# Attention beside an FFN: exponentiating and transposing each tile's probabilities in the step that rounds them, and splitting them one step behind

## The chip, the cores and the metric

One Trainium2 chip, one of its cores. The metric is the device time of one execution in microseconds (us), lower is better. The engines are TensorE (PE; its weight loads are PEld), VectorE (DVE), ScalarE (ACT), GpSimd (POOL) and SyncE (SP, which here only issues DMAs). Each engine runs its own queue of instructions in order and waits on semaphores for the others.

## The reference

Attention with a hash mask over 4 batches x 8 heads, 768 positions of 64 channels, whose result, all heads side by side, goes through an FFN of 512 -> 2048 -> 512 over 3072 tokens. All in float32.

```python
q_bits = (einsum('bhsd,dk->bhsk', q, proj) > 0)      # 6 bits per query, the same for keys
mask   = q_bucket[:, :, :, None] == k_bucket[:, :, None, :]
scores = where(mask, q @ k^T / sqrt(64), -1e9)
attn   = exp(scores - max(scores)); attn /= sum(attn) + 1e-9
x      = (attn @ v) as [3072, 512]
h      = x @ w_in
out    = (h * clip(h + 3, 0, 6) / 6) @ w_out
```

## The kernel before

The work of attention goes in 192 **steps** (`NS`), one for each tile of 128 queries of a head: 6 steps to a head (`KT`), 48 to a batch (`HK`). For tile `g`, in this order:

- `scores(g)` (L362, L364): 4 matmuls give the negated scores `s`, 128 queries x 768 keys, in PSUM. Products of float32 precision are made of rounded high and low parts; the hash bits ride along as extra rows, so that keys of another bucket get a huge value.
- `lowest(g)` (L371, DVE): one pass that caps `s`, writes it to the SBUF tile `p` and gives the row minimum `m`. There are two `p` tiles.
- `exponential(g)` (L383, ACT): `p = exp(m - p)` in place, with the row sum (a second instruction reads the accumulator).
- From step 106 on (`GT`) the tile is transposed by `flip(g)` and `move(g)`: a DVE transpose of 32 x 32 blocks in place (L404), a DMA of `p` to DRAM (`fd`), and four DMAs back that put the blocks in order, into one of two **homes**: the tile `spare` for even `g`, `px` for odd. Before step 106 TensorE transposes instead (`transp`, L393).
- `split_p(g, c, ...)` for the two halves c of the keys: a rounded copy `ph` (L450, ACT) and the rest `pl`, a subtraction of `ph` from the home. In these steps `pl` of c=0 is made by DVE (L454; both its inputs are in SBUF), `pl` of c=1 by POOL (L452).
- `values(u, c)` (L474, L475): 12 matmuls for a pair u of tiles, `ph` and `pl` with the head's `vv`, into `acc`; `output` copies `acc` to SBUF (L502; L499 and L500 for the last head of a batch) and sends it to the DRAM array `xs`.

The FFN of a chunk of 256 tokens runs as 16 **FFN steps**, one beside each attention step once its batch is done: `gemm1` (12 matmuls, L592 to L594) gives `h`; `gate` is a Relu on ACT (L612) and a product on DVE (L613); `split_g` makes `gh` (L620, ACT) and `gl` (L621, POOL); `gemm2` (6 matmuls, L630 to L632) adds into `po`. At a chunk's end its result is stored (L646) and the next chunk's `x` is normalised and split (L530, L540, L543, L583, L584).

PE, DVE, ACT and POOL run in the order in which the code is written (`tc.manual_schedule`); only the place of SP's DMAs is chosen by the framework. `beside_ffn(k)` writes step k of the paced part, k from 105 on. The FFN is a generator, and `go("A")` to `go("D")` let it write its next piece if that is its turn: A `split_g`, B `gemm1`, C `gemm2` of the FFN step before and then `gate`, D side work of the next chunk. Before the change step k writes: the values of a pair, `exponential(k+1)`, A, `split_p` of tile k - 2 (`LT = 2`), B, `lowest(k+2)`, `flip(k+1)`, `output`, in one step of six `hash_qk` and `bits` (the next head's hash, L316 to L318 and L327), C, `lead(k+3)` (scores, and loads and splits of the next head: L296, L304, L342, L343), the delayed DVE subtractions (`split_lows`), `move(k)`, D. `s` has one buffer, which the hash's `z` shares; `ph` and `pl` have two pairs; `fd` has four.

Of the kernel before, what the change touches and what calls it, by code (L numbers as in the profile page):

```python
# [28 lines left out]
LA = 3  # L29
FB = 4  # L30
FS = 4
FT = 6
LT = 2
WL = 30
WE = 8
WA = 4
# [7 lines left out]
def lsh_attention_moe(  # L44
# [14 lines left out]
    KT = S // P  # L59
# [16 lines left out]
    def dma(out: bass.AP, in_: bass.AP):  # L76
        nonlocal last
        last = nc.sync.dma_start(out=out, in_=in_)

    paced = False  # L80
# [146 lines left out]
    NJ = B * H  # L227
    NS = NJ * KT
# [3 lines left out]
    GT = GF + FT  # L232
# [133 lines left out]
    def lowest(g: int):  # L366

        s = scs.pop(g)
        m = sp.tile([P, 1], F32, name=f"m{g}", tag="m", bufs=4)
        pr_ = sp.tile([P, 2, HW], F32, name=f"p{g}", tag="p", bufs=2)  # L370
        nc.vector.tensor_scalar(  # L371
            out=pr_[:], in0=s[:, :, :HW], scalar1=CAP, scalar2=None,
            op0=ALU.min, op1=ALU.min, accum_out=m[:],
        )
        probs[g] = pr_, m

    def exponential(g: int):
        i, t = divmod(g, KT)
        b, h = divmod(i, H)
        if b not in sms:  # L380
            sms[b] = sp.tile([P, KT, H], F32, name=f"sms{b}", tag="sms", bufs=2)
        pr_, m = probs[g]
        nc.scalar.activation(  # L383
            pr_[:], pr_[:], AF.Exp, bias=m[:], scale=-1.0, accum_out=sms[b][:, t, h : h + 1]
        )
# [15 lines left out]
    def flip(g: int):  # L401
        nonlocal written
        x = probs.pop(g)[0][:].rearrange("p c k -> p (c k)")
        nc.vector.transpose(x, x)  # L404
        d = dp.tile([P, S], F32, name=f"fd{g}", tag="fd", bufs=4)
        dma(out=d[:], in_=x)
        written[g] = d, last
# [18 lines left out]
    def split_p(g: int, c: int, third: bool):  # L426

        nonlocal halves
        u, w = divmod(g, 2)
        if w == 0:  # L430
            extra = third and halves % 3 == 2
            halves += 1
            if extra and lent:
                both = [x[:, :S] for x in lent]
            else:
                both = [
                    sp.tile([P, NCC * TC if extra else S], F32R, name=f"{x}{u}_{c}", tag=f"x{x[1]}" if extra else x, bufs=1 if extra else 2)[:, :S]
                    for x in ("ph", "pl")
                ]
            parts[u, c] = [x.rearrange("p (x w q) -> p x w q", x=QT, w=2) for x in both]  # L440
        hi, lo = (x[:, :, w] for x in parts[u, c])
        engine = nc.vector
        if g < GT:
            pt = pts.pop((g, c))[:]
        else:
            pt = moved[g].rearrange("p (i x a) -> p x i a", i=4, x=KT)[:, c * QT : (c + 1) * QT]
            hi, lo = (x.rearrange("p x (i a) -> p x i a", i=4) for x in (hi, lo))
            if c:
                engine = nc.gpsimd
        nc.scalar.copy(hi, pt)  # L450
        if engine is nc.gpsimd:
            engine.tensor_sub(lo, pt, hi.bitcast(F32))  # L452
        else:
            lows.append(lambda: engine.tensor_sub(lo, pt, hi.bitcast(F32)))  # L454
# [3 lines left out]
    def split_lows():  # L458
        for f in lows:
            f()  # L460
        lows.clear()
# [87 lines left out]
    def multiply():  # L549
        for f in muls:  # L550
            f()
        muls.clear()
# [434 lines left out]
    vnext = 0  # L987
# [21 lines left out]
    with tc.manual_schedule(engines={ET.PE, ET.DVE, ET.Activation, ET.Pool}):  # L1009
        split_qk(0, None)  # L1010
        hash_qk(0)
        bits(0)
        scale_q(1)
        split_v(0)
        for x in range(3):
            ahead(0, x)
        for _ in range(2):
            cv(0)
        def go(part: str):
            if stage == part:  # L1020
                next(fill, None)

        through = []

        def beside_ffn(k: int):

            nonlocal paced, stage
            for c in range(2):  # L1030
                if k < GT:
                    transp(k, c)
            for _ in range(1 if k < GT else 2):
                u = vnext // 2
                if u < NS // 2 and (k < GT or k % 2 == 0 and k >= 2 * u + 2 + (LT if 2 * u >= GT else 0)):
                    if value_half():
                        through.append(vnext // 2 - 1)
            if k + 1 < NS:
                exponential(k + 1)
            go("A")  # L1040
            late = k if k < GT else k - LT
            if GT <= late < NS or k < GT:
                for c in range(2):
                    split_p(late, c, False)
            go("B")
            if k == NS + LT:
                homes.clear()
            if k + 2 < NS:
                lowest(k + 2)
            if k + 1 < NS:  # L1050
                flip(k + 1)
            paced = True
            multiply()
            while through and (through[0] < vnext // 2 - 1 or k % 2 or k < GT):
                output(through.pop(0))
            if k + LA < NS and (k + LA) % KT == 3 and (k + LA) // KT + 1 < NJ:
                hash_qk((k + LA) // KT + 1)
                bits((k + LA) // KT + 1)
            go("C")
            if k + LA < NS:  # L1060
                lead(k + LA)
            split_lows()
            if GT <= k < NS:
                move(k)
            if subs:
                subs.pop(0)()
            go("D")
            if k % KT in (2, 4):
                add()

        for k in range(NS + LT + 2):
            if k >= GT - 1:
                beside_ffn(k)
                continue
            end = GB if k < GB else NS
            i, t = divmod(k, KT)
            if k == HK - XE:
                lent += lents[cc3:]
            if k == GB:
                lent.clear()  # L1080
            if k == HK:
                late["x"] = sp.tile([P, S], F32, name="late", tag="raw", bufs=1)
            for c in range(2):
                transp(k, c)
            if k + 1 < end:
                exponential(k + 1)
            if k + 2 < end:
                lowest(k + 2)
            if k == GB:
                next(first)  # L1090
                pair_turn = 0

            third = True
            whole = False
            for _ in range(1 if k != HK else 2):
                if vnext < k - k % 2:
                    whole = value_half()
            if k >= GF - 2:
                next(fill, None)
            if whole and k >= GF:  # L1100
                output(vnext // 2 - 1)
                whole = False

            hashed = k >= GF and (k + LA) % KT == 2
            if k >= GF and k + LA < end and not hashed:
                lead(k + LA)
            for c in range(2):
                split_p(k, c, third)
            split_lows()
            if (k < GF or hashed) and k + LA < end:  # L1110
                if hashed:
                    if (k + LA) // KT + 1 < NJ:
                        hash_qk((k + LA) // KT + 1)
                        bits((k + LA) // KT + 1)
                    next(fill, None)
                lead(k + LA)
            if whole:
                output(vnext // 2 - 1)
            if k >= GF - 2 and not hashed:
                next(fill, None)  # L1120
            if k < GB:
                for f in early_steps[k]:
                    f()

            if k < HK and t == 1 and i:
                with tc.issue_after(last.ins):
                    load_w(i)
            if k == HK:
                late_x()
                with tc.issue_after(last.ins):  # L1130
                    get_qk(H + 2)
                    for n in range(WE, WL):
                        load_w(n)
            if k + 1 == GB:
                first = first_ffn(lambda part: ahead(GB, part))
                next(first)
                for _ in range(2):
                    whole = value_half()
                output(vnext // 2 - 1)
                next(first)  # L1140
        paced = False
        assert vnext == NS and not through
        add()
        for _ in fill:
            pass
# [47 lines left out]
```

## Time and profile before

| | |
|---|---|
| three runs | 1049.42, 1053.89 (median), 1058.02 us |
| the profiled execution | 1051.75 us, its span 1050.0 us |
| PE busy | 977.9 us, 93% of the span |
| DVE, ACT, POOL busy | 695.4, 637.3, 536.2 us |
| mean granted TensorE clock | 0.982 |
| the paced steps (first to last L404) | 416.3 to 864.0 us |
| DMA | 148.37 MB, mean 141 GB/s |

Busy time is not the whole cost: matmuls overlap, so their durations add up to more than the time from one issue to the next, and an instruction that is held by another engine's use of the memory shows as a longer one, not as a wait. In rows of the timeline the first number is the start, the second the duration, both in us, and in brackets stands how long the engine had been idle and what released it.

### The profile page before, as it was taken

The page shows a single profiled execution, that of the slowest core. Times are in us where ns is not written, and L with a number is a line of the kernel's source. Part 1 is how long each engine was busy: PE and PEld are TensorE (multiplying, and loading weights), DVE is VectorE, ACT ScalarE, POOL GpSimd, SP SyncE. Part 2 cuts the span into 40 slices and gives each one's busy share as a digit, 9 for nine tenths or more (in the row PEclk, how much of TensorE's full clock was granted, in tenths as well). Part 3 has the DMA queues.
Part 4 walks back from the last instruction along what each step waited for, and adds up shares of the span by engine and source line. Part 5 has one row for each costly group of instructions (what it writes and reads, how often), then busy time and mean ns, then how long its engine had stood idle before and what let it go on. Part 6 is the DMA issues. An engine that isn't in the chain of part 4 may idle for free.

```text
span 1050.0 us, 19259 instructions
## 1 busy us (share of the span) xinstructions
PE 977.9 (93%) x6330; PEld 883.7 (84%) x6330; DVE 695.4 (66%) x1350; ACT 637.3 (61%) x1419; POOL 536.2 (51%) x609
## 2 busy tenths in 40 slices
PE   8999999999999997898898898988889999999998
PEld 7999888888899997787788887877778888799997
DVE  7999988898499997566656665755655672233332
ACT  6889865555588886465656565655665574333332
POOL 6778725666367765456655555645665553200100
PEclk9999999999999999899999999999999999999999
DMA  4556587000244553677876777777786673101000
GB/s 127 145 143 168 149 275 273 1 1 1 75 124 113 115 129 93 201 214 204 230 209 190 210 197 212 195 215 205 204 238 189 185 214 84 41 1 41 1 21 21
DMA packets 109339, 148.37 MB, mean 141 GB/s; under 512 B 12804, under 2 KB 78724, under 8 KB 109240
## 3 DMA queue, kind: packets, MB, share of 16 engines
q1 hardware_dynamic: 104760, 141.64, 45.0%
q0 software_dynamic: 4480, 5.51, 4.7%
q8 instruction: 50, 0.82, 0.3%
q14 instruction: 49, 0.40, 0.1%
HBM read 75.76 MB, written 51.90 MB: 122 GB/s over the span
## 4 chain that ended last, share of the span: by engine, by line
PE 57%; DMA 16%; DVE 14%; issue 5%; ACT 3%; SPq 2%; POOL 2%; DVEq 0%; ACTq 0%; POOLq 0%
DMA fd<-p 9%; PE h L593 6%; PE h L592 6%; PE h L594 6%; PE pt L393 5%; PE po L632 4%; PE acc L475 4%; PE po L630 4%; PE acc L474 4%; DVE p L371 4%; PE po L631 4%; DVE pl L454 4%; DMA px<-fd 3%; PE s L364 3%; PE s L362 3%
## 5 line engine op out<-in xcount | busy, mean ns | idle before, releaser
L371 DVE TENSOR_SCALAR_CACHE_REDUCE p<-s 128x768 f32<-128x768 f32 x192 | 183.3, 955 | 156.7 <-DMA fd<-p 115.6
L383 ACT ACTIVATE p<-p,m 128x768 f32<-128x768 f32 x192 | 179.7, 936 | 30.2 <-DVE p L371 29.3
L612 ACT ACTIVATE g<-h,three 128x256 f32<-128x256 f32 x192 | 91.4, 476 | 157.6 <-PE h L594 137.3
L475 PE MATMUL acc<-pl,vv 128*128 128x256 f32 x564 | 147.2, 292 | 16.3 <-DVE pl L454 16.3
L613 DVE SCALAR_TENSOR_TENSOR g<-g,h 128x256 f32<-128x256 f32 x192 | 79.5, 414 | 123.1 <-ACT g L612 121.3
L474 PE MATMUL acc<-ph,vv 128*128 128x256 f32 x564 | 154.1, 303 | 3.2 <-DVE pl L454 3.1
L592 PE MATMUL h<-xh,w 128*128 128x256 f32 x512 | 147.1, 287 | 0.0
L594 PE MATMUL h<-xh,w 128*128 128x256 f32 x512 | 145.5, 284 | 0.0
L593 PE MATMUL h<-xl,w 128*128 128x256 f32 x512 | 145.5, 284 | 0.0
L621 POOL TENSOR_TENSOR gb<-g,gb 128x256 fp32r<-128x256 f32 x92 | 70.3, 764 | 127.1 <-ACT gb L620 125.3
L475 PEld LDWEIGHTS acc<-pl,vv 128*128 128x128 f32 x564 | 110.3, 196 | 21.9 <-DVE pl L454 21.6
L362 PE MATMUL s<-kk,qq 76*128 76x384 f32 x384 | 102.5, 348 | 15.0 <-DVE p L371 13.6
L474 PEld LDWEIGHTS acc<-ph,vv 128*128 128x128 f32 x564 | 109.5, 194 | 6.4 <-issue 2.2
L450 ACT CAST ph<-pt 128x384 fp32r<-128x384 f32 x204 | 91.4, 475 | 25.2 <-PE pt L393 13.7
L454 DVE TENSOR_TENSOR pl<-pt,ph 128x384 fp32r<-128x384 f32 x204 | 103.9, 549 | 3.0 <-ACT ph L450 2.5
L632 PE MATMUL po<-w,gb 128*128 128x512 f32 x248 | 100.4, 405 | 2.5 <-POOL gb L621 2.0
L630 PE MATMUL po<-w,gb 128*128 128x512 f32 x248 | 99.5, 401 | 2.5 <-ACT gb L620 2.5
L592 PEld LDWEIGHTS h<-xh,w 128*128 128x128 f32 x512 | 99.0, 193 | 1.6 <-DVE xr L543 0.2
L364 PE MATMUL s<-kk,qq 128*128 128x384 f32 x384 | 100.2, 342 | 0.0
L593 PEld LDWEIGHTS h<-xl,w 128*128 128x128 f32 x512 | 98.8, 193 | 1.6 <-DVE xl L584 0.2
L631 PE MATMUL po<-w,gb 128*128 128x512 f32 x248 | 98.6, 398 | 0.0
L594 PEld LDWEIGHTS h<-xh,w 128*128 128x128 f32 x512 | 98.6, 193 | 0.0
(164 smaller groups left out, 2398.1 us busy)
## 6 DMA issues: line engine op xcount, KB each, us to landing
fd<-p SPq DMA_DIRECT2D x86, 384.0 KB
spare<-fd SPq DMA_DIRECT2D x172, 96.0 KB
px<-fd SPq DMA_DIRECT2D x172, 96.0 KB
raw<-in_qkT SPq DMA_DIRECT2D x32, 384.0 KB
kk<-qq SPq DMA_DIRECT2D x62, 192.0 KB
wr<-in_w_in SPq DMA_DIRECT2D x16, 512.0 KB
wr<-in_w_out SPq DMA_DIRECT2D x16, 512.0 KB
vr<-in_v SPq DMA_DIRECT2D x32, 192.0 KB
```

Of the source, the lines that this page charges most:

```text
L362: nc.tensor.matmul(s[:, c, :HW], lhsT=q1[:KM, us], rhs=half(k1[:KM], c), start=True, stop=False)
L371: nc.vector.tensor_scalar(out=pr_[:], in0=s[:, :, :HW], scalar1=CAP, scalar2=None, op0=ALU.min, op1=ALU.min, accum_out=m[:],)
L383: nc.scalar.activation(pr_[:], pr_[:], AF.Exp, bias=m[:], scale=-1.0, accum_out=sms[b][:, t, h : h + 1])
L454: lows.append(lambda: engine.tensor_sub(lo, pt, hi.bitcast(F32)))
L474: nc.tensor.matmul(acc[:], lhsT=vv[:, kt], rhs=hi[:, x], start=(kt == 0), stop=False)
L475: nc.tensor.matmul(acc[:], lhsT=vv[:, kt], rhs=lo[:, x], start=False, stop=(kt == KT - 1))
L592: nc.tensor.matmul(hp[:], lhsT=wi[:, 0, wc], rhs=xh, start=(cc == 0), stop=False)
L593: nc.tensor.matmul(hp[:], lhsT=wi[:, 0, wc], rhs=xl, start=False, stop=False)
L594: nc.tensor.matmul(hp[:], lhsT=wi[:, 1, wc], rhs=xh, start=False, stop=(cc == NCC - 1))
L630: nc.tensor.matmul(po[u], lhsT=gh[:, us], rhs=wo[:, 0], start=(fc == 0), stop=False)
L631: nc.tensor.matmul(po[u], lhsT=gh[:, us], rhs=wo[:, 1], start=False, stop=False)
L632: nc.tensor.matmul(po[u], lhsT=gl[:, us], rhs=wo[:, 0], start=False, stop=(fc == NFC - 1))
```

## The change

In the paced part, step k now writes `lowest(k+2)`, `exponential(k+2)` and `flip(k+2)` one behind the other, ahead of B; `move(k+1)` instead of `move(k)`; and `split_p` of tile k - 1 (`LT = 1`), with its DVE subtraction in the same place instead of at the step's end. So a tile is rounded, exponentiated and transposed two steps ahead, read back a step sooner, and split one step behind the current one. The values of a pair are made on odd steps instead of even ones, `output` on even instead of odd, the hash on k % 6 == 5 instead of 0, and `bits` stands behind C. The loop has one iteration less.

```diff
-LT = 2
+LT = 1
...
-            for c in range(2):
-                if k < GT:
+            if k < GT:
+                for c in range(2):
                     transp(k, c)
-            for _ in range(1 if k < GT else 2):
+                exponential(k + 1)
+                flip(k + 1)
+            for _ in range(2):
                 u = vnext // 2
-                if u < NS // 2 and (k < GT or k % 2 == 0 and k >= 2 * u + 2 + (LT if 2 * u >= GT else 0)):
+                if u < NS // 2 and (2 * u < GT or k % 2 and k >= 2 * u + 3):
                     if value_half():
                         through.append(vnext // 2 - 1)
-            if k + 1 < NS:
-                exponential(k + 1)
+                if k < GT:
+                    break
             go("A")
+            if k + 2 < NS:
+                lowest(k + 2)
+                exponential(k + 2)
+            paced = True
+            multiply()
+            if k + 2 < NS:
+                flip(k + 2)
             late = k if k < GT else k - LT
             if GT <= late < NS or k < GT:
                 for c in range(2):
                     split_p(late, c, False)
+            split_lows()
             go("B")
             if k == NS + LT:
                 homes.clear()
-            if k + 2 < NS:
-                lowest(k + 2)
-            if k + 1 < NS:
-                flip(k + 1)
-            paced = True
-            multiply()
-            while through and (through[0] < vnext // 2 - 1 or k % 2 or k < GT):
+            while through and (through[0] < vnext // 2 - 1 or k % 2 == 0 or k < GT):
                 output(through.pop(0))
-            if k + LA < NS and (k + LA) % KT == 3 and (k + LA) // KT + 1 < NJ:
+            hashed = k + LA < NS and (k + LA) % KT == 2 and (k + LA) // KT + 1 < NJ
+            if hashed:
                 hash_qk((k + LA) // KT + 1)
+            go("C")
+            if hashed:
                 bits((k + LA) // KT + 1)
-            go("C")
             if k + LA < NS:
                 lead(k + LA)
-            split_lows()
-            if GT <= k < NS:
-                move(k)
+            if GT <= k + 1 < NS:
+                move(k + 1)
             if subs:
                 subs.pop(0)()
             go("D")
-            if k % KT in (2, 4):
+            if k % KT in (1, 3):
                 add()
```

In the rows below a number directly behind `p`, `m`, `s` or `fd` is the tile g, behind `ph` and `pl` the pair and then the half c; `g1_2_6` is FFN step 6 of a chunk. First VectorE's queue in steps 144 and 145, before:

```order
L371 TENSOR_SCALAR p146_8028,m146_8027<-s146_7980 128x768
L404 STREAM_TRANSPOSE p145_7960<-p145_7960 128x768
L327 TENSOR_SCALAR qq_25_7858<-z25_8033,thr_66,val_67 44x768
L613 SCALAR_TENSOR_TENSOR g1_2_6_8048<-g1_2_6_8048,h1_2_6_8014 128x256
L454 TENSOR_TENSOR pl71_0_8008<-spare_5400,ph71_0_8007 128x3x128
L371 TENSOR_SCALAR p147_8086,m147_8085<-s147_8055 128x768
L404 STREAM_TRANSPOSE p146_8028<-p146_8028 128x768
L500 TENSOR_TENSOR y23_0_7965<-acc70_7990,y23_0_7965 64x256
L613 SCALAR_TENSOR_TENSOR g1_2_7_8100<-g1_2_7_8100,h1_2_7_8072 128x256
L454 TENSOR_TENSOR pl71_0_8008<-px_5741,ph71_0_8007 128x3x128
```

And VectorE's queue at the same place after the change:

```order
L371 TENSOR_SCALAR p146_8032,m146_8031<-s146_8019 128x768
L404 STREAM_TRANSPOSE p146_8032<-p146_8032 128x768
L454 TENSOR_TENSOR pl71_0_7978<-px_5691,ph71_0_7977 128x3x128
L500 TENSOR_TENSOR y23_0_7932<-acc70_7954,y23_0_7932 64x256
L613 SCALAR_TENSOR_TENSOR g1_2_6_8064<-g1_2_6_8064,h1_2_6_8042 128x256
L371 TENSOR_SCALAR p147_8097,m147_8096<-s147_8071 128x768
L404 STREAM_TRANSPOSE p147_8097<-p147_8097 128x768
L454 TENSOR_TENSOR pl72_0_8104<-spare_5400,ph72_0_8103 128x3x128
L613 SCALAR_TENSOR_TENSOR g1_2_7_8130<-g1_2_7_8130,h1_2_7_8111 128x256
```

The transpose is now of the tile that the instruction ahead of it wrote (146 behind 146), and the subtraction L454 has moved from the step's end to right behind the transpose; it belongs to one tile later.

ScalarE's queue in the same two steps, before:

```order
L383 ACTIVATE p145_7960,sms3_7938<-p145_7960,m145_7959 128x768
L620 CAST gb1_2_5_8004<-g1_2_5_7974 128x256
L450 CAST ph71_0_8007<-spare_5400 128x3x128
L450 CAST ph71_1_8010<-spare_5400 128x3x128
L612 ACTIVATE g1_2_6_8048<-h1_2_6_8014,three_68 128x256
L383 ACTIVATE p146_8028,sms3_7938<-p146_8028,m146_8027 128x768
L620 CAST gb1_2_6_8066<-g1_2_6_8048 128x256
```

And ScalarE's queue after the change:

```order
L620 CAST gb1_2_5_8028<-g1_2_5_8011 128x256
L383 ACTIVATE p146_8032,sms3_7910<-p146_8032,m146_8031 128x768
L450 CAST ph71_0_7977<-px_5691 128x3x128
L450 CAST ph71_1_7980<-px_5691 128x3x128
L499 COPY y23_0_7932<-acc70_7954 64x256
L612 ACTIVATE g1_2_6_8064<-h1_2_6_8042,three_68 128x256
L620 CAST gb1_2_6_8093<-g1_2_6_8064 128x256
```

The exponential is of tile 146 where it was of 145, it stands behind the gate's cast instead of ahead of it, and the two copies `ph` follow it directly.

SyncE's queue at steps 144 and 145, before:

```order
L78 DMA fd145_8031<-p145_7960 128x768
L78 DMA kk_25_7857<-qq_25_7858 12x768
L78 DMA spare_5400<-fd144_7963 32x4x192 x4
L78 DMA fd146_8089<-p146_8028 128x768
L78 DMA xs2_127<-y23_0_7965 64x512
L78 DMA px_5741<-fd145_8031 32x4x192 x4
```

And SyncE's queue after the change:

```order
L78 DMA fd146_8036<-p146_8032 128x768
L78 DMA xs2_127<-y23_0_7932 64x512
L78 DMA px_5691<-fd145_7975 32x4x192 x4
L78 DMA xr2_0_8245<-xs2_127 128x4x256
L78 DMA fd147_8101<-p147_8097 128x768
```

In both the write of a tile is followed by the four reads of the tile before it; writes and reads are one tile further on in the same step.

## The prediction

> **What bounds the kernel now.** I read the page first, then the stage that the diff touches. The stretches view and the group of the on-chip transposes (line 404) show where that stage lies and how dense it is.
>
> ```profile
> 416.00:864.00 448.00, 399.75 (x2448) 358.27 (x2448) 276.22 (x481) 266.83 (x601) 252.04 (x276) 0.96 0.72 206
> ```
> ```profile
> L404 DVE STREAM_TRANSPOSE p<-p x86: 966/973/979, 416.3 to 864.0; 128x768 f32<-128x768 f32 x86
> ```
>
> In the stretches row, behind the length stand the busy times of PE, PEld, DVE, ACT and POOL, then the granted clock, the DMA share and GB/s. The 86 steps beside the FFN lie between 416.3 and 864.0, 85 intervals in 447.7 us, 5.27 us a step. No engine is full there: PE is busy 399.75 of 448 us at a granted clock of 0.96. So a wait sets the pace, and the view of waits and the chain of that stretch name it.
>
> ```profile
> DVE p L371 <- DMA fd<-p: 115.6, 55, 5.4
> ```
> ```profile
> by line: DMA fd<-p 19.7%; issue 7.5%; DMA px<-fd 7.1%; DVE p L371 5.2%; DVE p L404 5.1%; SPq L78 5.1%; DMA spare<-fd 3.9%; DVE pl L454 3.8%; PE acc L475 3.3%; PE h L593 3.0%; PE h L592 3.0%; PE h L594 3.0%; PE po L632 2.8%; PE po L630 2.7%;
> ```
>
> The largest wait of VectorE is `lowest` (L371) on the landing of an earlier step's probabilities in DRAM, and that transfer is the largest piece of the chain. VectorE's own rows show why:
>
> ```profile
> 601.95 0.96 DVE L371 TENSOR_SCALAR_CACHE_REDUCE p<-s 128x768 f32<-128x768 f32 x1 [1.24 <-DMA fd<-p]
> 602.84 0.08 DVE L371 DVE_READ_ACCUMULATOR p<-s 128x1 f32 x1
> 602.84 0.97 DVE L404 STREAM_TRANSPOSE p<-p 128x768 f32<-128x768 f32 x1
> 604.53 0.42 DVE L613 SCALAR_TENSOR_TENSOR g<-g,h 128x256 f32<-128x256 f32 x1 [0.72 <-ACT g L612]
> 604.87 0.55 DVE L454 TENSOR_TENSOR pl<-spare,ph 128x384 fp32r<-128x384 f32 x1
> 606.34 0.96 DVE L371 TENSOR_SCALAR_CACHE_REDUCE p<-s 128x768 f32<-128x768 f32 x1 [0.93 <-DMA fd<-p]
> 607.23 0.08 DVE L371 DVE_READ_ACCUMULATOR p<-s 128x1 f32 x1
> 607.23 0.97 DVE L404 STREAM_TRANSPOSE p<-p 128x768 f32<-128x768 f32 x1
> 608.12 0.38 DVE L613 SCALAR_TENSOR_TENSOR g<-g,h 128x256 f32<-128x256 f32 x1
> ```
>
> There are two `p` buffers. `lowest(k+2)` writes the one that `flip(k)` gave to the DMA a step ago. So one step is a loop: `lowest` 0.89, `flip` 0.97, then 606.34 - 603.81 = 2.53 us until the transfer has landed, together 4.39 us, and more whenever the transfer stands behind others (the mean is 5.27).
>
> **The change part by part.** No instruction is added or removed. What it does to that loop: `flip(k+2)` now stands in the step of `lowest(k+2)`, so the buffer that `lowest(k+2)` needs was given away two steps ago. Two steps of 4.5 us and more stand against 0.89 + 1.06 + 0.97 + 2.53 = 5.45 us of `lowest`, exponential, `flip` and landing. I cost this wait at nothing afterwards. Its cover is some 3.5 us beyond an ordinary landing (waits of 0.93 and 1.24 in the rows); only one like the longest, 5.4, would come through, with under 1 us. The question is what is late next. That is a new chain inside a step: `lowest` waits for the scores, the exponential for `lowest`, `flip` for the exponential, and behind `flip` on VectorE queue the low part of the probabilities (`pl`, L454), the gate (L613), bits, and the next `lowest`. For its times:
>
> ```profile
> 605.13 0.92 ACT L383 ACTIVATE p<-p,m 128x768 f32<-128x768 f32 x1
> 605.96 0.19 ACT L383 ACTIVATION_READ_ACCUMULATOR p<-p,m 128x1 f32 x1
> 606.05 0.39 ACT L620 CAST gb<-g 128x256 fp32r<-128x256 f32 x1
> 606.34 0.93 ACT L450 CAST ph<-px 128x384 fp32r<-128x384 f32 x2
> ```
> ```profile
> 606.53 0.73 POOL L621 TENSOR_TENSOR gb<-g,gb 128x256 fp32r<-128x256 f32 x1 [1.65 <-ACT gb L620]
> ```
> ```profile
> 618.41 0.08 DVE L371 DVE_READ_ACCUMULATOR p<-s 128x1 f32 x1
> ...
> 618.53 0.94 ACT L383 ACTIVATE p<-p,m 128x768 f32<-128x768 f32 x1 [0.16 <-DVE p L371]
> ```
>
> Count from the exponential's start. It ends with its accumulator read at 605.96 + 0.19 - 605.13 = 1.02. A handoff between DVE and ACT takes 618.53 - 618.49 = 0.04 (I take it in both directions), so `flip` starts at 1.06 and the next VectorE instruction, `pl` for c=0, can start 608.12 - 607.23 = 0.89 later, at **1.95**. On ScalarE the two copies `ph` (L450) follow the exponential at 0.92 and end 0.93 later; POOL starts 606.53 - 606.44 = 0.09 after ScalarE ends (0.08 in other rows), so its `pl` for c=1 (L452) starts at 1.93 to **1.94**. Before, these two subtractions stood at different ends of the step. Now they start together, POOL some 0.02 us ahead. What two such instructions do to each other is in two pairs of rows:
>
> ```profile
> 511.59 1.81 POOL L304 TENSOR_TENSOR kk<-raw,qq 64x768 fp32r<-64x768 f32 x1 [0.40 <-POOL pl L452]
> 511.62 2.20 DVE L454 TENSOR_TENSOR pl<-px,ph 128x384 fp32r<-128x384 f32 x1
> ```
> ```profile
> 554.27 1.44 POOL L343 TENSOR_TENSOR vv<-vr,vv 128x384 fp32r<-128x384 f32 x1
> ...
> 554.29 0.54 DVE L454 TENSOR_TENSOR pl<-px,ph 128x384 fp32r<-128x384 f32 x1
> ```
>
> With POOL 0.03 ahead, VectorE's instruction lasted until 0.42 after POOL's end (513.40, 513.82). With POOL 0.02 ahead, VectorE was not held at all, and POOL's took 0.44 longer than its usual 1.00. One of the two is held for the other's whole length, and the lead that decides lies between 0.02 and 0.03 us, just where the change puts it. A rule of the Trainium skill speaks against this change here: in "SBUF — State Buffer", section "Who interferes with whom", a VectorE instruction with two SBUF inputs contends with a GpSimd instruction that reads SBUF, and "Issue order, not op shape, decides who blocks." The trace agrees on the blocking (0.42 after POOL's end); on the order, the second pair shows a start 0.02 us later that still won. By the rule alone every step goes to POOL, the first rival below; by the two pairs, not every one.
>
> The pace follows from a loop of two steps: pl of an even step, the 12 value matmuls of the next (they are late by this change only where pl is), gemm1, gemm2, the scores, and `lowest` again.
>
> ```profile
> 600.92 0.28 PE L474 MATMUL acc<-ph,vv 128*128 128x256 f32 x1
> ...
> 602.36 0.28 PE L592 MATMUL h<-xh,w 128*128 128x256 f32 x1
> ...
> 605.86 0.28 PE L592 MATMUL h<-xh,w 128*128 128x256 f32 x1
> ```
> ```profile
> L452 POOL TENSOR_TENSOR pl<-px,ph 128x384 fp32r<-128x384 f32 x42 | 43.8, 1042 | 9.3 <-ACT ph L450 4.1 <-DMA spare<-fd 2.9
> ```
>
> The values take 602.36 - 600.92 = 1.44 (0.12 each), a step's gemm1, gemm2 and scores 605.86 - 602.36 = 3.50. The last scores end 0.16 after the next issue (0.28 - 0.12). From `lowest` to the exponential are 0.97 + 0.04 = 1.01.
>
> **POOL first:** POOL's pl ends at 1.93 + 1.02 = 2.95, VectorE's at 3.37; handoff 0.04, 11 value matmuls 1.32, then 3.50, 0.16, 0.04 and 1.01: the exponential of the next even step starts at 9.44, **4.72 a step**. VectorE's own ring (pl to 3.37, the gate 0.34, `lowest` 1.01, less the 0.08 by which its instructions overlap) is 4.64, just under it.
>
> **VectorE first:** its pl ends at 2.50, POOL's at about 2.95 + 0.44 = 3.39; the last five value matmuls wait for that: 3.43 + 0.60 + 3.50 + 0.16 + 0.04 + 1.01 = 8.74, **4.37 a step**. That is PE's own 3.50 + 0.72 = 4.22 and little more.
>
> One pair in three also has the next head's hash, whose bits stand before the scores.
>
> ```profile
> L327 DVE TENSOR_SCALAR qq<-z,thr,val 44x768 fp32r<-44x768 f32 x13 | 14.1, 1086 | 12.7 <-PE z L318 12.7
> ```
>
> POOL first, the odd step's gate is issued through at 4.64 + 3.63 = 8.27, bits end at 9.36, and the scores (0.72, by the rows' x384 matmuls an estimate: 2 x 0.36), 0.16, two handoffs and 1.01 end at 11.33. VectorE first, the six hash matmuls, 1.08 by the same estimate, go through PE: 8.74 + 1.08 = 9.82. Three pairs: 2 x 9.44 + 11.33 = 30.2, **5.04** a step, or 2 x 8.74 + 9.82 = 27.3, **4.55**.
>
> To both I add 0.2 a step for what stays: the ends of FFN chunks put `xl`, reciprocals and stores on the same ring. The row for `xl`:
>
> ```profile
> L584 DVE TENSOR_TENSOR xl<-xr,xh 128x256 fp32r<-128x256 f32 x12 | 10.2, 878 | 1.0 <-ACT xh L583 1.0
> ```
>
> That is 10.2 us over 85 steps, 0.12; with the smaller things (reciprocals, the last heads' additions, stores) I estimate 0.2. Over 85 steps: POOL first 5.24, 445 us, 2 us less than now; VectorE first 4.75, 404 us, 44 less.
>
> The other edits cost nothing under this cover: `output` moves to even steps, where ScalarE's 0.3 fits before the held gate; the hash moves to odd steps, whose PE has the time that the loop leaves; values and splits a step sooner keep their distance of one step; the loop is one iteration shorter, but that FFN step is only done afterwards. ScalarE's exponential now waits for `lowest`, and the copies, the gate's relu and so gemm2 queue behind it; that wait is in the rings. On SP the four reads of `move(k+1)` still stand behind the write of the step's own `flip`, and wait for the subtractions that free their home; the path home is the slow rival below.
>
> **The forecast.** The lead is too small to name one winner for all steps; I take POOL first in two steps of three: (2 x 2 + 44) / 3 = 16 us. The profiled execution took 1051.75 us (its span 1050.0), which gives 1036; the median shown is 1053.89, 2 above it, so **1038**.
>
> **The rivals.** *POOL always first:* the start times alone decide, 1.93 against 1.95. 2 us less than now, 1052. For it: the first pair of rows, and that POOL leads in these sums; against it: the second pair. The rule of the Trainium skill in "SBUF — State Buffer" gives this case. *VectorE (nearly) always first:* 44 less, 1010. For it: a handoff on ScalarE or POOL only 0.01 longer. *Slower:* the way home becomes the bound. A home is free at 3.37, four issues on SP and the landing follow, and `ph` two steps on must find the data.
>
> ```profile
> 610.64 2.00 SPq L78 DMA_DIRECT2D px<-fd  x4
> ...
> 616.55 0.93 ACT L450 CAST ph<-px 128x384 fp32r<-128x384 f32 x2 [2.37 <-DMA px<-fd]
> ```
>
> Here the landing came 616.55 - 612.64 = 3.9 after the issues. It may take 2 x 5.24 + 0.92 - 3.37 - 2.00 = 6.0 before ScalarE waits; in the step where three transfers of the next head stand ahead on SP, about 2 less. If it takes 6 there, it costs 2 us in each of 14 heads, 28 in all, and with POOL first 1080; against it: nothing in the rows is that long. *The wait stays* because the landings grow with the traffic (DMA share 0.72 now): 1054.
>
> **How the numbers follow.** Chances: forecast, with some of each, 0.42 (1028 to 1048); POOL always 0.25 (1046 to 1058); VectorE always 0.23 (1003 to 1028); the wait stays 0.04; slower 0.06 (above 1064). One per cent, about what a measurement of this kernel can tell from no change, is 10.5 us: faster means below 1043.4. That is three quarters of the forecast, all of VectorE first and a little of POOL first: 0.58; slower 0.07; the same 0.35. The range 1007 to 1058 leaves out part of the low case and the slow one.
>
> **What would show it.** L371's idle before it on `fd<-p` nearly gone; instead L404 waiting for ACT L383 about 1 us in each of 86 steps, and L371 for the scores. L454's times in two heaps, 0.55 and about 1.4, with L452's the other way round (1.5 and 1.0): the share of heaps tells which case it is. The step 4.75 to 5.24 us; PE's clock nearer 1. I am wrong if L454 stays at 0.55 and the step is still over 5, or if ScalarE's `ph` waits for `px` or `spare`.

## The result and the profile after

The changed kernel takes **1016.55 us** (median of four runs, 1015.21 to 1016.7) against 1054.83 of the kernel before beside it: ratio 0.9639, 95% interval 0.9598 to 0.9681, faster by 38 us. The prediction was 1038 with a gain of 16; the direction is right, the time lies in the range of 1007 to 1058, and the gain is more than twice the one forecast. It is the rival "VectorE (nearly) always first", to which the prediction gave 1010 us and a chance of 0.23.

The profiled execution took 1015.21 us. Where its 36.5 us less come from (1051.75 before): the stretch of the 86 paced steps, 413.4 to 830.1, is 416.7 us long (447.7 before), 31.0 less; it starts 2.9 earlier; and what follows it in the span takes 183.3 instead of 186.0. A step takes 4.90 us instead of 5.27. The row of the transposes and the stretches view of that stretch, with the columns as before (PE, PEld, DVE, ACT, POOL busy, then clock, DMA share, GB/s):

```profile
L404 DVE STREAM_TRANSPOSE p<-p x86: 966/978/981, 413.4 to 830.1; 128x768 f32<-128x768 f32 x86
```
```profile
413.00:830.00 417.00, 389.87 (x2466) 349.78 (x2467) 275.54 (x483) 263.95 (x605) 285.84 (x280) 0.99 0.76 222
```

PE is now busy for 93% of it (89% before), the clock is 0.99, and POOL is busier by 34 us than in the 448 us of before, with 280 instructions against 276: its instructions have become longer. The waits from 410 to 840 us (us in total, times, longest):

```profile
POOL pl L452 <- ACT ph L450: 95.2, 62, 2.7
DVE p L404 <- ACT p L383: 86.5, 85, 1.4
ACT p L383 <- DVE p L371: 82.6, 76, 2.7
DVE p L371 <- PE s L364: 46.2, 53, 1.1
...
PE po L632 <- POOL gb L621: 16.3, 17, 1.5
```

The wait of `lowest` (L371) on `fd<-p`, 115.6 us before, is gone from the list. `flip` (L404) now waits for the exponential about 1 us in each step, and `lowest` waits for the scores: PE leads. So says the chain of that stretch, where DMA `fd<-p` had the first place with 20%:

```profile
by line: issue 10.3%; PE acc L475 7.2%; PE po L632 7.1%; PE acc L474 5.9%; PE h L593 5.6%; PE h L594 5.4%; PE h L592 5.3%; PE po L630 5.2%; PE po L631 5.2%; PE s L362 5.0%; POOL pl L452 5.0%; PE s L364 4.8%; DMA px<-fd 3.3%; POOL gb L621 3.
```

The question that the prediction left open, which of the two `pl` holds the other, is answered by their groups (ns min/median/max, first and last start):

```profile
L454 DVE TENSOR_TENSOR pl<-spare,ph x43: 515/517/562, 428.1 to 838.9; 128x384 fp32r<-128x384 f32 x43
```
```profile
L452 POOL TENSOR_TENSOR pl<-spare,ph x43: 1009/1437/1448, 428.1 to 839.3; 128x384 fp32r<-128x384 f32 x43
```

VectorE's takes 0.517 in the median, POOL's 1.437 where its own time is 1.02: POOL is the held one. Yet POOL starts first, as a plain step shows:

```profile
641.49 0.94 ACT L383 ACTIVATE p<-p,m 128x768 f32<-128x768 f32 x1 [0.41 <-DVE p L371]
...
642.55 0.98 DVE L404 STREAM_TRANSPOSE p<-p 128x768 f32<-128x768 f32 x1 [0.76 <-ACT p L383]
643.41 1.43 POOL L452 TENSOR_TENSOR pl<-spare,ph 128x384 fp32r<-128x384 f32 x1 [1.37 <-ACT ph L450]
643.45 0.52 DVE L454 TENSOR_TENSOR pl<-spare,ph 128x384 fp32r<-128x384 f32 x1
```

From the exponential's start it is 1.92 us to POOL's `pl` and 1.96 to VectorE's (predicted: 1.94 and 1.95). POOL's stamp is 0.036 to 0.045 us ahead in 73 of the 86 steps, and VectorE's wins all of them. In four of the other steps VectorE's is the held one (1.69 to 2.19 us).

PE leads, but not alone. In a plain pair of steps the values still wait for both `pl`:

```profile
582.63 1.43 POOL L452 TENSOR_TENSOR pl<-px,ph 128x384 fp32r<-128x384 f32 x1 [1.67 <-ACT ph L450]
582.67 0.52 DVE L454 TENSOR_TENSOR pl<-px,ph 128x384 fp32r<-128x384 f32 x1
...
583.24 0.39 PE L475 MATMUL acc<-pl,vv 128*128 128x256 f32 x1 [0.20 <-DVE pl L454]
...
584.11 0.39 PE L475 MATMUL acc<-pl,vv 128*128 128x256 f32 x1
```

The first matmul with `pl` starts 0.05 us after VectorE's has ended, the fourth 0.05 us after POOL's has.

### The profile page after: what moved, and what is told of

The parts are those of the page before. It is cut to its first block, busy times and chain, and to the rows that moved or that the text cites. A ratio compares the mean times of both kernels' runs of the same rounds, so it can differ in the third digit from the quotient of the medians.

```text
span 1013.4 us, 19291 instructions
## 1 busy us (share of the span) xinstructions
PE 966.4 (95%) x6330; PEld 874.2 (86%) x6330; DVE 695.9 (69%) x1350; ACT 633.6 (63%) x1419; POOL 565.0 (56%) x609
## 4 chain that ended last, share of the span: by engine, by line
PE 65%; DVE 13%; issue 7%; POOL 6%; ACT 5%; DMA 3%; SPq 1%; DVEq 0%; POOLq 0%; ACTq 0%
PE acc L475 6%; PE h L593 6%; PE po L632 6%; PE h L594 6%; PE h L592 6%; PE acc L474 6%; PE po L630 5%; PE pt L393 5%; PE po L631 5%; PE s L362 4%; PE s L364 4%; DVE pl L454 3%; DVE p L371 2%; POOL pl L452 2%; ACT ph L450 2%
## 5 line engine op out<-in xcount | busy, mean ns | idle before, releaser
L371 DVE TENSOR_SCALAR_CACHE_REDUCE p<-s 128x768 f32<-128x768 f32 x192 | 183.1, 954 | 63.0 <-PE s L364 48.2
L474 PE MATMUL acc<-ph,vv 128*128 128x256 f32 x564 | 151.9, 299 | 3.9 <-DVE pl L454 3.7
L613 DVE SCALAR_TENSOR_TENSOR g<-g,h 128x256 f32<-128x256 f32 x192 | 80.5, 419 | 106.0 <-ACT g L612 103.2
L592 PE MATMUL h<-xh,w 128*128 128x256 f32 x512 | 145.2, 284 | 0.0
L594 PE MATMUL h<-xh,w 128*128 128x256 f32 x512 | 143.6, 280 | 0.0
L404 DVE STREAM_TRANSPOSE p<-p 128x768 f32<-128x768 f32 x86 | 84.1, 978 | 86.5 <-ACT p L383 86.5
L632 PE MATMUL po<-w,gb 128*128 128x512 f32 x246 | 99.5, 404 | 16.4 <-POOL gb L621 16.3
L475 PEld LDWEIGHTS acc<-pl,vv 128*128 128x128 f32 x564 | 107.8, 191 | 7.2 <-DVE pl L454 5.1
L474 PEld LDWEIGHTS acc<-ph,vv 128*128 128x128 f32 x564 | 107.4, 190 | 7.1 <-PE pt L393 2.0
L454 DVE TENSOR_TENSOR pl<-pt,ph 128x384 fp32r<-128x384 f32 x204 | 104.0, 549 | 3.0 <-ACT ph L450 2.5
L620 ACT CAST gb<-g 128x256 fp32r<-128x256 f32 x139 | 56.4, 406 | 79.3 <-DVE g L613 45.4
L593 PEld LDWEIGHTS h<-xl,w 128*128 128x128 f32 x512 | 96.6, 189 | 6.7 <-DVE xl L584 3.0
L216 POOL TENSOR_TENSOR w<-wr,w 128x128 fp32r<-128x128 f32 x128 | 73.6, 607 | 47.4 <-ACT w L210 47.2
L592 PEld LDWEIGHTS h<-xh,w 128*128 128x128 f32 x512 | 96.6, 189 | 1.7 <-ACT xh L583 0.3
L630 PE MATMUL po<-w,gb 128*128 128x512 f32 x246 | 97.6, 397 | 0.0
## 6 DMA issues: line engine op xcount, KB each, us to landing
wr<-in_w_out SPq DMA_DIRECT2D x16, 512.0 KB, 10.9
```

The costliest lines, as they stand in the source:

```text
L371: nc.vector.tensor_scalar(out=pr_[:], in0=s[:, :, :HW], scalar1=CAP, scalar2=None, op0=ALU.min, op1=ALU.min, accum_out=m[:],)
L474: nc.tensor.matmul(acc[:], lhsT=vv[:, kt], rhs=hi[:, x], start=(kt == 0), stop=False)
L475: nc.tensor.matmul(acc[:], lhsT=vv[:, kt], rhs=lo[:, x], start=False, stop=(kt == KT - 1))
L592: nc.tensor.matmul(hp[:], lhsT=wi[:, 0, wc], rhs=xh, start=(cc == 0), stop=False)
L593: nc.tensor.matmul(hp[:], lhsT=wi[:, 0, wc], rhs=xl, start=False, stop=False)
L594: nc.tensor.matmul(hp[:], lhsT=wi[:, 1, wc], rhs=xh, start=False, stop=(cc == NCC - 1))
```

## Experiments

The theory after the result: **(1)** the wait for the `p` buffer is gone, the pace is the loop over two steps through `pl` of c=0, and the change gains so much because VectorE wins the meeting of the two `pl`. Its rivals: **(2)** that meeting matters little, and the whole gain is the removed wait; **(3)** the gain is in other parts of the change. Each ratio is against runs of the kernel before on the same chip (medians of 1051.74 to 1054.25 us). "Pair" is the time of two steps, from the starts of L371. Where a line is added near the top, the later lines' numbers are one higher.

### A very short instruction ahead of VectorE's pl (late_pl), and its control (late_gate)

```diff
+    nil = cp.tile([P, 1], F32, name="nil")
...
                     split_p(late, c, False)
+            if lows:
+                nc.vector.memset(nil[:], 0.0)
             split_lows()
```

The control has the same memset behind `split_lows()`.

> The changed kernel with one short VectorE instruction (a memset of one column of a scratch tile) between the on-chip transpose and the subtraction pl of c=0, so that this subtraction starts some 0.06 us later. In the changed kernel POOL's pl of c=1 starts 0.04 us ahead of it and yet is the one that is held (1.43 us instead of 1.0). Theory 1, the start decides and only a lead of over 0.04 us lets POOL win: with a lead of 0.1 us VectorE's subtraction is held, about 1.4 us instead of 0.52, POOL's takes 1.0, the step goes from 4.90 to about 5.25 us, 30 us more in all, about 1045 us. Theory 2, VectorE wins such a meeting whatever the start: subtractions as they are, at most 0.06 us a step more, under 5 us in all, about 1018 us.

> The control: the same short VectorE instruction, but behind the subtraction pl of c=0, so that the two subtractions meet as in the changed kernel. Both theories: pl of c=0 0.52 us, pl of c=1 1.43 us, the time 0 to 5 us over that of the changed kernel, 1016 to 1022 us.

late_pl: 1041.73 us, ratio 0.9879 [0.985, 0.9908]. late_gate: 1020.1 us, 0.9674 [0.9644, 0.9704]. The same 87 memsets of 0.06 us each, in one place or the other, differ by 21.6 us. The timeline of late_pl:

```profile
631.44 1.01 POOL L453 TENSOR_TENSOR pl<-px,ph 128x384 fp32r<-128x384 f32 x1 [1.52 <-ACT ph L451]
631.49 1.37 DVE L455 TENSOR_TENSOR pl<-px,ph 128x384 fp32r<-128x384 f32 x1
631.51 0.06 DVE L1056 MEMSET nil<- 128x1 f32 x1
```

Now POOL's takes 1.01 and VectorE's lasts until 0.41 after POOL's end. The medians over all steps are 1.012 and 1.378; in late_gate they are 1.434 and 0.517, as in the changed kernel. Plain pairs take 4.6 + 4.9 = 9.5 us (9.44 predicted for POOL first), against 3.86 + 4.96 = 8.8 in the changed kernel and in late_gate; the paced steps 443.6 us (445 predicted for POOL first). Theory 1 holds, 2 falls: of the 38 us, 22 to 25 hang on who wins this meeting.

### VectorE's pl back at the step's end (pl_at_end)

```diff
                     split_p(late, c, False)
-            split_lows()
             go("B")
...
                 lead(k + LA)
+            split_lows()
```

> The changed kernel with the VectorE subtraction pl of c=0 put back behind the gate and the scores, where it stood before; the rest as changed. If the meeting of the two subtractions costs time even when VectorE wins: POOL's pl back to 1.0 us, 0.43 us less of POOL in each of 86 steps, gl earlier, 5 to 15 us less than the changed kernel, 1000 to 1012 us. If it costs nothing, because POOL has the time: within 5 us of the changed kernel, and VectorE's subtraction meets POOL's splits of the next head instead (some of its 86 at over 1 us).

1041.5 us, 0.9882 [0.9847, 0.9917]: a miss. The two do not meet and POOL's `pl` takes its own 1.02 again, but that buys nothing, since VectorE's now ends about 3.4 us after the exponential's start in the even steps. The values' matmuls with `pl` wait for it; in the changed kernel that row has 0.2 us, once:

```profile
PE acc L475 <- DVE pl L454: 25.0, 28, 1.6
```

Plain pairs take 4.33 + 5.25 = 9.6, about the same as when VectorE loses the meeting (9.5), where its `pl` ends at 3.35. So what a plain pair follows here is when `pl` of c=0 ends. Whether POOL's longer `pl` costs something beside it, this run does not separate.

### Only the two steps ahead (two_ahead), and all but that (loop_kept)

two_ahead is the kernel before with this alone:

```diff
+            if k < GT:
+                exponential(k + 1)
+                flip(k + 1)
...
-            if k + 1 < NS:
-                exponential(k + 1)
             go("A")
...
+            if k < GT:
+                split_lows()
             go("B")
...
             if k + 2 < NS:
                 lowest(k + 2)
-            if k + 1 < NS:
-                flip(k + 1)
+                exponential(k + 2)
             paced = True
             multiply()
+            if k + 2 < NS:
+                flip(k + 2)
```

loop_kept is the changed kernel with the exponential of tile k + 1 again ahead of A, its flip right behind `lowest(k+2)`, and `move(k)`.

> The kernel before with one part of the change alone: lowest, exponential and flip of tile k+2 one behind the other; move(k), the split two steps behind and the subtraction at the step's end stay (only at the first paced step the subtraction is made at once). If the loop over the two p buffers was what bounded the kernel, this alone brings nearly all of the gain: the wait of lowest for the write to DRAM goes from 116 us to under 10, and the time is 1010 to 1025 us. If the earlier read and split are needed as well (the chain through the homes bounds next), the waits of ph on spare and px grow and the time stays over 1035 us.

> The changed kernel without its first part: the exponential and flip are of tile k+1 again, as before, ahead of A and behind lowest(k+2), and move(k) reads back the tile of the step; the split one step behind, the subtraction right behind flip and the values on odd steps stay. Theory 1, the loop over the two p buffers bounds whatever else is moved: lowest waits for the write to DRAM over 80 us again and the time is 1040 to 1065 us. Theory 2, the earlier split is what gained: 1015 to 1030 us.

two_ahead: 1047.19 us, 0.9941 [0.9917, 0.9965]. loop_kept: 1065.69 us, 1.011 [1.0067, 1.0154]. Waits of two_ahead (its profiled execution was its slowest, 1053.46):

```profile
ACT ph L450 <- DMA px<-fd: 30.6, 16, 5.4
...
DVE p L371 <- DMA fd<-p: 1.7, 2, 1.0
...
PE acc L475 <- DVE pl L454: 33.1, 32, 3.0
```

The wait for `p` is down from 115.6 to 1.7 us, and the kernel gains 6: with `pl` at the step's end and the split two steps behind, the loop through `pl` and the way home take its place. In loop_kept the first loop is still there (61.4 us of wait, less than the 80 expected), and the tile is wanted a step sooner, so that the way home holds the copies `ph` for longer still:

```profile
ACT ph L450 <- DMA spare<-fd: 79.0, 32, 4.3
ACT ph L450 <- DMA px<-fd: 70.8, 39, 4.6
DVE p L371 <- DMA fd<-p: 61.4, 41, 3.1
```

So one part alone gives -6 us, the rest alone +11 (`move` being left out of both), all together -38. Neither gains much without the other: theory 3 is half right, the "other parts" carry the gain only once the wait is gone.

### The split between `lowest` and the exponential (split_early)

```diff
+            late = k if k < GT else k - LT
+            early = GT <= late < NS
             if k + 2 < NS:
                 lowest(k + 2)
+            if early:
+                for c in range(2):
+                    split_p(late, c, False)
+                split_lows()
+            if k + 2 < NS:
                 exponential(k + 2)
...
-            late = k if k < GT else k - LT
-            if GT <= late < NS or k < GT:
+            if k < GT:
                 for c in range(2):
                     split_p(late, c, False)
```

> The changed kernel with split_p (both copies ph on ScalarE and both subtractions pl) between lowest(k+2) and exponential(k+2), where ScalarE waits about 1 us for lowest and VectorE about 1 us for the exponential. Theory 1, the pace is the loop pl, values, gemm1, gemm2, scores, lowest: pl ends some 1.5 us earlier, the loop falls under PE's own work, plain pairs of steps go from 8.9 to 8.4-8.6 us, the two subtractions do not hold each other (POOL's 1.0 us, VectorE's 0.52), and the time is 995 to 1008 us. Theory 2, in odd steps the copies wait for the values that still read the ph tiles, the exponential stands behind them, and the chain of the step grows by up to 1 us there: pairs of 8.9 us and more, 1015 to 1030 us.

1030.73 us, 0.9773 [0.9737, 0.981]: slower than the changed kernel. Plain pairs did what was expected (3.5 + 4.9 = 8.4), but the steps with the next head's hash took 6.6 to 8.1 and ends of chunks up to 11, because the copies stand ahead of the exponential and now wait for the landing, and for the values that still read the `ph` tiles (second row):

```profile
ACT ph L450 <- DMA spare<-fd: 28.5, 9, 6.4
...
ACT ph L450 <- PE acc L474: 18.4, 38, 2.0
...
PE s L362 <- DVE qq L327: 15.4, 9, 3.7
ACT ph L450 <- DMA px<-fd: 15.3, 16, 1.8
```

So the exponential, and all that follows it, waits with the copies here.

### POOL's half first (c1_first)

```diff
-                for c in range(2):
+                for c in ((1, 0) if k >= GT else (0, 1)):
                     split_p(late, c, False)
```

> The changed kernel with the copies ph in the other order, c=1 ahead of c=0, so that POOL's pl of c=1 starts 0.45 us ahead of VectorE's pl of c=0 instead of 0.04. Both theories of the meeting: POOL wins, 1.0 us, and VectorE is held about 0.55 us (1.0 in all). If what costs is only where pl of c=0 ends (2.95 us behind the exponential's start, against 2.5 now and 3.4 in the run with POOL first): pairs of about 9.0 us and a time of 1015 to 1028 us, nearer to the changed kernel than to the 1042 us of that run. If it costs as much as there to be held at all: over 1035 us.

1028.81 us, 0.975 [0.9703, 0.9796], just above the 1015 to 1028 expected. POOL starts 0.45 us ahead and wins every step:

```profile
L454 DVE TENSOR_TENSOR pl<-px,ph x43: 966/980/1705, 433.8 to 853.9; 128x384 fp32r<-128x384 f32 x43
```

VectorE's `pl` ends 2.95 us after the exponential's start, and plain pairs take 4.2 + 4.9 = 9.1 (9.0 expected). Three points of one line: `pl` of c=0 ends at 2.48, 2.95, 3.35, and a pair takes 8.8, 9.1, 9.5. The last 0.4 of delay costs 0.4; the first 0.47 only 0.3. In the changed kernel the values wait for POOL's `pl` too (the rows above), which ends at 3.36 there and at 2.52 here.

### POOL's low parts of the next head cut in two (halves)

The steps before the hash take 4.9 us in the changed kernel where a plain one takes 3.9. Its timeline there:

```profile
685.32 1.85 POOL L304 TENSOR_TENSOR kk<-raw,qq 64x768 fp32r<-64x768 f32 x1
...
687.10 0.85 POOL L481 DMA_DIRECT2D xs<-y  x1
688.01 0.72 POOL L621 TENSOR_TENSOR gb<-g,gb 128x256 fp32r<-128x256 f32 x1
...
688.79 0.51 PE L632 MATMUL po<-w,gb 128*128 128x512 f32 x1 [1.12 <-POOL gb L621]
```

`gl` (L621) stands behind the next head's L304 and the issue of a store on POOL, and PE waits 1.12 us for it. The experiment cuts L304 in two and spreads the pieces:

```diff
             if paced:
-                subs.append(low)
+                for c in (slice(0, HW), slice(HW, S)):
+                    subs.append(lambda to=to, r=r, c=c: nc.gpsimd.tensor_sub(to[:, c], raw[r, c], q1[r, c].bitcast(F32)))
...
             go("A")
+            if subs:
+                subs.pop(0)()
```

> The changed kernel with POOL's two splits of the next head (L304, 1.85 us each) cut into four halves, one at a step's end and one behind gl of the next step. If POOL, with its pl at 1.43 us, is what makes the pair of steps with the hash 11.1 us (9.8 were worked out), because gl stands behind these splits: PE's wait of its third gemm2 matmul for gl goes from 16 us to under 6, the hash pair to 10.3 or less, the time to 1004 to 1012 us. If the hash pair is long for another reason: within 4 us of the changed kernel, 1013 to 1021 us.

1012.37 us, 0.9599 [0.9563, 0.9636]. The wait named above is halved (8.0 us instead of 16.3; under 6 was expected):

```profile
PE po L632 <- POOL gb L621: 8.0, 17, 0.7
```

Hash pairs without a chunk's end take 4.1 + 6.3 to 6.6 in most heads, 10.4 to 10.6 instead of 10.9 to 11.1: the step before the hash loses 0.8 us, the one with it gives back about 0.3. The mechanism is shown by the wait; that the kernel is faster than the changed one by its 4 us is not, since they were not run beside each other and the intervals of their ratios overlap.

### The early split in even steps only (even_early), and both (even_halves)

```diff
-            early = GT <= late < NS
+            early = GT <= late < NS and k % 2 == 0
```

This is split_early with that line, and with the old place for odd steps; even_halves adds the edit of halves.

> The run with the split between lowest and the exponential gave plain pairs of 3.5 + 4.9 us, as the loop has it, but its steps with the hash took 6.6 to 8.1 us instead of 6.2, with the exponential behind copies that wait for the values or for the read of the tile. Here the split is early in even steps alone, the steps whose pl the loop holds; odd steps, the hash's among them, split as in the changed kernel. If it is so: plain pairs 8.4 to 8.6 us, hash steps 6.0 to 6.4, 996 to 1010 us. If the early split costs in even steps too (the read of px is then late): pairs near 8.9, over 1014 us.

> The same with POOL's splits of the next head in four halves, which took 4 us off the changed kernel. If the two add up: 4 us less than the run with the early split in even steps alone, 992 to 1006 us. If the early split takes away what the halves won (POOL's pl is no longer held by VectorE in even steps, so gl is in time anyway): the same time as that run within 3 us.

even_early: 1020.26 us, 0.9695 [0.9678, 0.9712]; even_halves: 1010.35 us, 0.96 [0.9584, 0.9616], the fastest version measured. In even_early many plain pairs are at 8.4, but VectorE's early `pl` now meets other POOL instructions, `gl` among them, and `gl` is later still (first row); even_halves, on the same chip, is 10 us faster than it, where 4 or nothing was expected, and its wait is 9.5 us shorter (second row). even_early itself was expected at 996 to 1010 us: a miss.

```profile
PE po L632 <- POOL gb L621: 20.9, 19, 2.2
```
```profile
PE po L632 <- POOL gb L621: 11.4, 17, 1.3
```

Against the changed kernel the 6 us of even_halves are again not shown, for the intervals of the two ratios overlap.

### What decides the meeting (tiny_sub, tiny_copy)

```diff
+            if lows:
+                nc.vector.tensor_sub(nil[:], three[:], three[:])
             split_lows()
```

tiny_copy has `nc.vector.tensor_copy(nil[:], three[:])` in that place.

> The changed kernel with a subtraction of one column (128x1, both inputs in SBUF) on VectorE between flip and its pl, where late_pl had a memset of one column. Theory A: what counts is when VectorE's pl itself starts; the extra instruction puts it back as the memset did (the memset was stamped 0.06 us long, and pl's stamp moved from 1.964 to 1.972 us after the exponential's start). Then POOL wins as in late_pl: L452's shift 1.01 us, VectorE's pl about 1.38, plain pairs 9.5 us, time 1037 to 1046. Theory B: the memory is taken by the first VectorE instruction with two inputs in SBUF and kept while the next follows directly, as in the rows where VectorE's pl follows another pl and starts 0.05 us behind POOL and is not held. Then the small subtraction takes it in pl's old place: VectorE's pl stays at 0.52, POOL's at 1.43 or a little more, plain pairs 8.9 to 9.1, time 1015 to 1024.

> The same with a copy of one column (128x1, one input in SBUF) in place of the subtraction. Both theories: POOL wins as in late_pl (VectorE's pl about 1.38 us, POOL's 1.01, plain pairs 9.5, 1037 to 1046), if only an instruction with two inputs in SBUF takes the memory; if any reading instruction does, VectorE wins and the time is 1015 to 1024.

tiny_sub: 1043.48 us, 0.9907 [0.9877, 0.9937]; tiny_copy: 1042.94 us, 0.9904 [0.9872, 0.9935]. Both are theory A. In tiny_sub:

```profile
636.91 1.04 POOL L453 TENSOR_TENSOR pl<-spare,ph 128x384 fp32r<-128x384 f32 x1 [1.53 <-ACT ph L451]
636.95 0.12 DVE L1056 TENSOR_TENSOR nil<-three 128x1 f32<-128x1 f32 x1
636.98 1.38 DVE L455 TENSOR_TENSOR pl<-spare,ph 128x384 fp32r<-128x384 f32 x1
```

The small subtraction starts 0.04 behind POOL, just where `pl` stood in the changed kernel, and is not visibly held; POOL's `pl` is 0.03 longer than in late_pl (medians 1.042 and 1.012). But the big one behind it loses. If the small one took the memory, of which those 0.03 us are the only sign, VectorE did not keep it for the next; POOL got in between. Theory B falls. The rows that it was drawn from do not bear on it either: there VectorE subtracts from `pt`, which is in PSUM, and neither instruction is longer than alone (0.55 on VectorE, 1.01 on POOL).

## Where the prediction failed, and where it was right

- **The bound before, and its removal: right.** The wait on `fd<-p` went from 115.6 us to nothing, and two_ahead, which does only that, leaves 1.7.
- **"The question is what is late next" and the loop through `pl`: right.** With `pl` late, the loop gave 9.5 us a pair in late_pl (9.44 predicted) and again in pl_at_end; the two cases of the sum, 445 and 404 us for 85 steps, were measured as 443.6 (late_pl) and 416.7. That the first fits so well is in part luck: late_pl's hash pairs took 11.6 (11.33 predicted) and its plain pairs 9.51, 6 us more in all, and the allowance for the ends of chunks was too large by about 7.
- **The meeting of the two `pl`: foreseen, its outcome not.** This is the step that failed: "I take POOL first in two steps of three". VectorE was first in all 73 steps where POOL's stamp was 0.036 to 0.045 us ahead, and that meeting is worth 22 to 25 us (late_pl). The start times were right to 0.02 us, and that one instruction holds the other too, but not "the lead that decides lies between 0.02 and 0.03 us". That bound came from two rows in which VectorE's `pl` follows the gate (L613) and meets other POOL instructions (L304, L343). Behind `flip` VectorE's still wins at 0.045; in late_pl it loses at 0.045 to 0.052. No one lead of the stamps fits all the rows. Whether the instruction ahead on VectorE shifts it, or the one on POOL, is not shown: in loop_kept VectorE's `pl` behind `flip` lost once to `gl` (L621) at 0.042. With the right winner the same sum gives 1010.
- **The rule of the Trainium skill** ("SBUF — State Buffer", section "Who interferes with whom") that the order of issue decides would have given 1052, with the stamped starts taken for that order. By the stamps it does not come out: POOL is 0.041 us ahead in the changed kernel and loses, 0.048 ahead in late_pl and wins. Since no trace here shows when an instruction is issued, the rule itself is neither confirmed nor refuted. That one of the two blocks the other agrees: POOL's takes 1.437 where its own time is 1.02.
- **POOL first was too slow as well.** The prediction's 1052 for it was 1041.73 in late_pl: 4 us come off the paced steps instead of 2, and 6.7 outside them, for which the sum had nothing.
- **VectorE first was too low by 6.5 us.** Plain pairs: 8.8 measured, 8.74 predicted. Hash pairs: 11.1 against 9.82. There the step with the hash did grow by about the 1.08 us of the sum (5.0 to 6.2), but the step before it by 1 us as well, because `gl` stands behind L304 and a store's issue on POOL, which the sum did not have (halves shows it). Over some 14 hash pairs and 28 plain ones that is +18 and +2 us. The allowance of 0.2 a step for ends of chunks, 17 us, was too large by about 7 (416.7 less 14.2 x 11.1 and 28.3 x 8.82 leaves 9.5). Outside the paced steps 5.6 us were gained that the sum did not have either; no run here shows why. That 1010 lies so near 1016.55 is in part luck, since these errors cancel.
- **The slow rival, the way home: not seen** in the changed kernel (`ph` on `spare` 3.6 us in all, on `px` 1.6), but it is near: with the copies 1.3 us earlier and more (split_early) `ph` waits for `spare` up to 6.4 us at a time.
- **"The other edits cost nothing under this cover": right only under it.** Alone they cost 11 us (loop_kept).

## What to carry to other kernels

When a change removes the largest wait, work out the next loop with its own times, and test it by doing that part alone: here it gave 6 of 38 us, and the rest came only with the moves that looked free. Where two instructions of VectorE and POOL will start within 0.05 us of each other, give both cases their price and do not weigh them by stamps from places where other instructions stand around them. Once such a kernel is tuned, treat that meeting as part of the design: one instruction of 0.06 us in the wrong place cost 22 us.

## What the hardware showed that was not expected

- The stamped starts of VectorE's instructions overlap and need not follow the order of its queue. `pl` is stamped 0.07 to 0.08 us before `flip` ends, in the changed kernel and in late_pl alike; in late_pl the memset, which is ahead of it in the queue, has the later stamp (631.51 against 631.49). The memset moved `pl`'s stamp by 0.008 us only, from 1.964 to 1.972, and turned the outcome in nearly every step. At which point of an instruction the memory is taken stays open.
- Which one is held shows in these rows as a longer instruction, not as a wait: 1.437 instead of 1.02 us on POOL, 1.378 instead of 0.517 on VectorE. POOL's busy time in the stretch rose from 252 to 286 us in this way; the values' wait for its `pl` is the part of the cost that the rows show.
